# A two-pass channel-gating kernel: one load queue instead of two, and six rows kept in leftover SBUF

## The chip, the cores and the metric

The kernel runs on one core of a Trainium2 chip. The metric is the device time of one execution in microseconds (us), lower is better. A trace's span, from its first to its last instruction, is about 1.7 us shorter than the time of that execution. Executions fall into a fast and a slow state.

Names: PE is the matrix engine, DVE the vector engine, ACT the scalar engine, POOL and SP two more engines. SP and ACT issue the DMA transfers, each on a queue of its own. HBM is the memory outside the core; SBUF and PSUM are the memories on it. A queue's transfers are cut into packets, which the trace records one by one. "The trace's landing events" are the sixteen semaphore increments that end a transfer, one for each DMA engine; a transfer has landed with the last of them.

## The reference, cut to what matters

```python
def reference(x, w_down, w_up):          # x: (1, 256, 256, 384) bf16, 50.33 MB
    s = x.mean(axis=(1, 2))              # one mean per channel
    s = sigmoid(silu(s @ w_down) @ w_up) # w_down (384, 24), w_up (24, 384)
    return x * s[:, None, None, :]
```

No output element is known before all of x has been read, and x does not fit in SBUF. So some of x must be read twice.

## The kernel before

x is cut into 64 chunks of 1024 pixels: 128 partitions, 8 rows of 384 channels each, 0.786 MB. SBUF has room for 33 chunk buffers.

Pass 1 loads every chunk, and PE adds it to a running sum with eight matmuls against a matrix of ones. Even chunks are loaded by SP, odd ones by ACT. A buffer is loaded again when PE is done with it.

```python
# SP: even chunks (ACT has the same loop with range(1, NCH, 2))
for i in range(0, NCH, 2):
    b = bufof[i]                                  # i % 33
    if i >= nbuf:
        sp.wait_ge(sem_MM, i - nbuf + 1)          # PE has done with chunk i - 33
    sp.dma_start(bufs[b][:], x_rows(i, 0, K)).then_inc(sem_Lb[b], 16)
# ... ACT: the last chunk, 63, comes in two transfers, 6 rows and 2 rows (sem_LB)

# PE, strictly in the order of the chunks
pe.wait_ge(sem_G, 1); pe.wait_ge(sem_W, 32)       # weights; three small transposes
# ... three matmuls into ps_wT ...
for i in range(NCH):
    pe.wait_ge(sem_Lb[bufof[i]], 16 * load_cnt_at[i])
    for j in range(K):
        # ... at row 6 of the last chunk: pe.wait_ge(sem_LB, 16)
        mm = pe.matmul(ps_sum[:], ones_sb[:], bufs[b][:, j * C:(j + 1) * C], ...)
    mm.then_inc(sem_MM, 1)
```

Then six small steps on DVE, ACT and PE make the gate s. Pass 2 multiplies and stores: first the 33 chunks still in SBUF ("resident", 31 to 63), then chunks 0 to 30, each reread into a buffer whose store has landed. The first resident chunk goes out in quarters, so that the first store starts early.

```python
# SP: rereads
for j, i in enumerate(streamed2):                 # chunks 0..30
    sp.wait_ge(sem_STb[b], 16 * done_val[order2[j]])
    sp.dma_start(bufs[b][:], x_rows(i, 0, K)).then_inc(sem_Lb[b], 16)
# DVE: one multiply per unit; ACT: one store per unit
for (i, r0, r1) in units:
    # ... wait for the reread, if chunk i is one
    dve.tensor_tensor(buf3d(b, r0, r1), buf3d(b, r0, r1), s_bcast(r1 - r0), ALU.mult).then_inc(sem_MUL, 1)
```

Of the kernel before, what the change touches and what calls it, by code (L numbers as in the profile page):

```python
# [5 lines left out]

_MAX_BUFS = None
_K = 8


def bass_standalone__se_block__vision_kernel(
# [36 lines left out]
    with ExitStack() as ctx:  # L48
# [6 lines left out]
        def sem(name):  # L55
            return ctx.enter_context(nc.semaphore(name))
# [39 lines left out]
        def buf3d(n, r0=0, r1=K):  # L96
            return bufs[n][:].rearrange("p (k c) -> p k c", c=C)[:, r0:r1, :]

        def s_bcast(nrow):
            return s_sb[:].unsqueeze(1).to_broadcast([P, nrow, C])  # L100

        bufof = {i: i % nbuf for i in range(NCH)}
        resident = list(range(NCH - nbuf, NCH))
        streamed2 = list(range(0, NCH - nbuf))
        order2 = resident + streamed2
        buf2 = {}
        for i in resident:
            buf2[i] = bufof[i]
        for j, i in enumerate(streamed2):
            buf2[i] = buf2[order2[j]]  # L110

        last_split = K - 2 if NCH > 1 else K
        first2 = order2[0]
        p2_pieces = {i: [(0, K)] for i in order2}
        p2_pieces[first2] = [(r, r + K // 4) for r in range(0, K, K // 4)]

        lcnt = [0] * nbuf
        load_cnt_at = {}
# [9 lines left out]
            for (r0, r1) in p2_pieces[i]:  # L128
                units.append((i, r0, r1))
        scnt = [0] * nbuf  # L130
        store_cnt_after_unit = []
        for (i, r0, r1) in units:
            scnt[buf2[i]] += 1
            store_cnt_after_unit.append(scnt[buf2[i]])
        total_stores = list(scnt)
        done_val = {}
        n = 0
        for i in order2:
            n += len(p2_pieces[i])
            done_val[i] = store_cnt_after_unit[n - 1]  # L140

        last = NCH - 1

        with nc.Block() as block:

            @block.sync
            def _(sp):
                for i in range(0, NCH, 2):
                    b = bufof[i]
                    if i >= nbuf:  # L150
                        sp.wait_ge(sem_MM, i - nbuf + 1)
                    if i == last:
                        sp.dma_start(
                            buf3d(b, 0, last_split), x_rows(i, 0, last_split)
                        ).then_inc(sem_Lb[b], 16)
                        sp.dma_start(
                            buf3d(b, last_split, K), x_rows(i, last_split, K)
                        ).then_inc(sem_LB, 16)
                    else:
                        sp.dma_start(bufs[b][:], x_rows(i, 0, K)).then_inc(sem_Lb[b], 16)  # L160
                for j, i in enumerate(streamed2):
                    b = buf2[i]
                    sp.wait_ge(sem_STb[b], 16 * done_val[order2[j]])
                    sp.dma_start(bufs[b][:], x_rows(i, 0, K)).then_inc(sem_Lb[b], 16)

            @block.gpsimd
            def _(pool):
# [11 lines left out]
            @block.vector  # L179
            def _(dve):  # L180
                dve.memset(ones_sb[:], 1.0).then_inc(sem_C, 1)  # L181
                dve.memset(dummy_sb[:], 0.0).then_inc(sem_C, 1)  # L182

                dve.wait_ge(sem_MM, NCH)
                dve.wait_ge(sem_WT, 1)
                dve.tensor_tensor_reduce(  # L186
                    out=zscr_sb[:],
                    in0=wdnT_sb[:],
                    in1=ps_sum[0:R, :],
                    scale=inv_npix,  # L190
                    scalar=0.0,
                    op0=ALU.mult,
                    op1=ALU.add,
                    accum_out=z_sb[:],
                ).then_inc(sem_V2A, 1)
                dve.wait_ge(sem_A2V, 1)
                dve.tensor_scalar(  # L197
                    hb_sb[:], ones_sb[0:R, :], z_sb[:, 0:1], sig_sb[:, 0:1],
                    ALU.mult, ALU.mult,
                ).then_inc(sem_V2P, 1)  # L200

                dve.wait_ge(sem_A2V, 2)
                for (i, r0, r1) in units:
                    b = buf2[i]
                    if i in reread_cnt_at and r0 == 0:
                        dve.wait_ge(sem_Lb[b], 16 * reread_cnt_at[i])
                    dve.tensor_tensor(  # L207
                        buf3d(b, r0, r1), buf3d(b, r0, r1), s_bcast(r1 - r0), ALU.mult
                    ).then_inc(sem_MUL, 1)

            @block.tensor
            def _(pe):
                pe.wait_ge(sem_G, 1)
                pe.wait_ge(sem_W, 32)
                for c in range(CT):
                    mm = pe.matmul(  # L216
                        ps_wT[c][:], wdn_sb[:, c * R:(c + 1) * R], ident_sb[:],
                        start=True, stop=True,
                    )
                mm.then_inc(sem_T, 1)  # L220

                pe.wait_ge(sem_C, 2)
                for i in range(NCH):
                    b = bufof[i]
                    pe.wait_ge(sem_Lb[b], 16 * load_cnt_at[i])
                    nrow = last_split if i == last else K
                    for j in range(K):
                        if i == last and j == nrow:
                            pe.wait_ge(sem_LB, 16)
                        mm = pe.matmul(  # L230
                            ps_sum[:],
                            ones_sb[:],
                            bufs[b][:, j * C:(j + 1) * C],
                            start=(i == 0 and j == 0),
                            stop=(i == last and j == K - 1),
                        )
                    mm.then_inc(sem_MM, 1)

                pe.wait_ge(sem_V2P, 1)
                pe.matmul(  # L240
                    ps_u[:], hb_sb[:], wup_sb[:], start=True, stop=True
                ).then_inc(sem_P2A, 1)

            @block.scalar
            def _(act):
                act.dma_start(  # L246
                    wdn_sb[:].rearrange("p (k r) -> p k r", r=R),
                    w_down.rearrange("(k p) r -> p k r", p=P),
                ).then_inc(sem_W, 16)
                act.dma_start(wup_sb[:], w_up).then_inc(sem_W, 16)  # L250

                act.wait_ge(sem_C, 2)
                act.activation(dummy_sb[:, 1:2], dummy_sb[:, 0:1], ACT.Sigmoid)  # L253

                wdnT_done = [False]

                def emit_wdnT_copies():
                    act.wait_ge(sem_T, 1)
                    for c in range(CT):
                        ins = act.activation(  # L260
                            wdnT_sb[:, c * P:(c + 1) * P], ps_wT[c][:], ACT.Copy
                        )
                    ins.then_inc(sem_WT, 1)
                    wdnT_done[0] = True

                for i in range(1, NCH, 2):
                    b = bufof[i]
                    if i >= nbuf:
                        act.wait_ge(sem_MM, i - nbuf + 1)
                    if i == last:  # L270
                        act.dma_start(
                            buf3d(b, 0, last_split), x_rows(i, 0, last_split)
                        ).then_inc(sem_Lb[b], 16)
                        act.dma_start(
                            buf3d(b, last_split, K), x_rows(i, last_split, K)
                        ).then_inc(sem_LB, 16)
                    else:
                        act.dma_start(bufs[b][:], x_rows(i, 0, K)).then_inc(sem_Lb[b], 16)  # L278
                    if i == 7:
                        emit_wdnT_copies()  # L280
                if not wdnT_done[0]:
                    emit_wdnT_copies()

                act.wait_ge(sem_V2A, 1)
                act.activation(sig_sb[:], z_sb[:], ACT.Sigmoid).then_inc(sem_A2V, 1)  # L285

                act.wait_ge(sem_P2A, 1)
                act.activation(s_sb[:], ps_u[:], ACT.Sigmoid).then_inc(sem_A2V, 1)  # L288

                for n, (i, r0, r1) in enumerate(units):  # L290
                    b = buf2[i]
                    act.wait_ge(sem_MUL, n + 1)
                    act.dma_start(o_rows(i, r0, r1), buf3d(b, r0, r1)).then_inc(
                        sem_STb[b], 16
                    )
                for b in range(nbuf):
                    act.wait_ge(sem_STb[b], 16 * total_stores[b])

# [27 lines left out]
```

## Time and profile before

| | before |
|---|---|
| median time | 314.18 us (5 runs, 313.87 to 314.45) |
| span of the trace | 312.7 us |
| moved by DMA | 125.17 MB: 50.33 read, 24.4 read again, 50.33 written |
| end of the sum on PE | 128.4 us |
| first multiply of pass 2 | 130.5 us |

These lines are from the page of the kernel before: the busy tenths of the DMA engines and the rate in 40 equal slices of 7.8 us, then what was moved.

```profile
DMA  7999999999999998189999999999999999999997
GB/s 267 423 420 415 418 417 419 414 417 417 418 415 418 418 417 337 45 289 412 424 423 425 420 428 425 424 426 422 428 425 424 426 422 428 425 424 426 422 428 320
DMA packets 23914, 125.17 MB, mean 400 GB/s; under 512 B 3020, under 2 KB 3684, under 8 KB 23908
HBM read 74.75 MB, written 50.33 MB: 400 GB/s over the span
```

The DMA engines are full in both passes, at about 417 GB/s in pass 1 and 425 in pass 2, with a hole in slices 16 to 18. So time is bytes over rate, plus the hole. The hole is the only place where compute matters.

The chain of waits across the hole (start in us, length in us, what):

```profile
121.69 0.05 issue
121.73 6.69 PE ps_sum L230 x40
128.42 0.02 issue
128.44 0.54 DVE zscr_sb L186
...
129.99 0.50 ACT s_sb L288
130.49 0.02 issue
130.51 5.30 DVE xbuf L207 x6
```

The windows view of the kernel before: stretch in us, its length, busy time of PE, PE's weight load, DVE, ACT and POOL (with counts), granted PE clock, DMA share, GB/s.

```profile
120.00:125.00 5.00, 4.00 (x26) 2.19 (x25) 0.00 (x0) 0.00 (x0) 0.00 (x0) 1.00 0.75 297
125.00:128.50 3.50, 3.41 (x21) 1.85 (x19) 0.06 (x1) 0.00 (x0) 0.00 (x0) 1.00 0.01 5
128.50:131.00 2.50, 0.33 (x1) 0.09 (x1) 1.28 (x5) 0.69 (x2) 0.00 (x0) 1.00 0.00 0
134.50:138.00 3.50, 0.00 (x0) 0.00 (x0) 3.50 (x3) 0.00 (x0) 0.00 (x0) 0.50 0.86 248
```

DMA is all but done by 125 us, but PE works on, without a pause, to 128.4: forty matmuls in a row, five whole chunks, after the landing at 121.69. PE is not slow. Forty matmuls took 6.69 us; less the extra length of the last one (0.33 us from start to end, against a pitch of 0.163), that is 0.163 us each and 1.31 us to a chunk, while a chunk takes DMA 1.88 us. It is late because of what it had to wait for.

### The profile page before, as it was taken

How to read it: one execution, taken by the hardware profiler on the slowest of the kernel's cores; microseconds unless marked ns; L12 is line 12 of the kernel's file. 1: busy time of each engine (PE TensorE's matmuls, PEld its weight loads, DVE VectorE, ACT ScalarE, POOL GpSimd, SP SyncE). 2: the span in 40 equal slices, each digit the busy share in tenths (PEclk: the TensorE clock that was granted, in tenths of full speed). 3: DMA queues.
4: the chain of work that ended last, by engine and by line, in shares of the span. 5: the costliest groups of instructions: out<-in, count | busy, mean ns of one | idle time of the engine just before them, and what ended most of it. 6: DMA issues, size and time to landing. Idle time of an engine off the chain costs nothing.

```text
span 312.7 us, 1327 instructions
## 1 busy us (share of the span) xinstructions
PE 90.6 (29%) x516; PEld 48.2 (15%) x516; DVE 109.0 (35%) x72; ACT 2.8 (1%) x7; POOL 0.5 (0%) x5
## 2 busy tenths in 40 slices
PE   0777577777777777400000000000000000000000
PEld 0334333443443334200000000000000000000000
DVE  0000000000000000499999999999555540000000
ACT  1000000000000000000000000000000000000000
POOL 0000000000000000000000000000000000000000
PEclk9999999999999999955555555555555555555555
DMA  7999999999999998189999999999999999999997
GB/s 267 423 420 415 418 417 419 414 417 417 418 415 418 418 417 337 45 289 412 424 423 425 420 428 425 424 426 422 428 425 424 426 422 428 425 424 426 422 428 320
DMA packets 23914, 125.17 MB, mean 400 GB/s; under 512 B 3020, under 2 KB 3684, under 8 KB 23908
## 3 DMA queue, kind: packets, MB, share of 16 engines
q10 hardware_dynamic: 14836, 75.54, 58.7%
q1 hardware_dynamic: 9072, 49.55, 38.6%
q8 instruction: 4, 0.07, 0.1%
q14 instruction: 2, 0.02, 0.0%
HBM read 74.75 MB, written 50.33 MB: 400 GB/s over the span
## 4 chain that ended last, share of the span: by engine, by line
DMA 53%; DVE 26%; PE 2%; ACTq 1%; ACT 0%; issue 0%
DMA xbuf<-in_x_dram 39%; DVE xbuf L207 25%; DMA out_dram<-xbuf 12%; PE ps_sum L230 2%; DMA wup_sb<-in_w_up_dram 2%; ACTq L278 1%; DVE zscr_sb L186 0%; ACT wdnT_sb L260 0%; ACT s_sb L288 0%; PE ps_wT L216 0%; ACTq L246 0%; PE ps_u L240 0%; DVE hb_sb L197 0%; ACT sig_sb L285 0%; DVE z_sb L186 0%
## 5 line engine op out<-in xcount | busy, mean ns | idle before, releaser
L207 DVE TENSOR_TENSOR xbuf<-xbuf,s_sb 128x3072 bf16<-128x3072 bf16 (+1 forms) x67 | 108.0, 1679 | 20.4 <-DMA xbuf<-in_x_dram 19.4
L230 PE MATMUL ps_sum<-xbuf,ones 128*128 128x384 bf16 x512 | 89.9, 330 | 30.8 <-DMA xbuf<-in_x_dram 30.8
L230 PEld LDWEIGHTS ps_sum<-xbuf,ones 128*128 128x128 bf16 x512 | 47.9, 98 | 72.5 <-DMA xbuf<-in_x_dram 42.6
L186 DVE CUSTOM_DVE_ANT_0 zscr_sb<-wdnT_sb,ps_sum 24x384 f32<-24x384 bf16 x1 | 0.5, 542 | 127.4 <-PE ps_sum L230 127.4
L216 PE MATMUL ps_wT<-ident,wdn_sb 128*24 128x128 bf16 x3 | 0.5, 298 | 7.4 <-DMA wup_sb<-in_w_up_dram 7.4
L216 PEld LDWEIGHTS ps_wT<-ident,wdn_sb 128*24 128x24 bf16 x3 | 0.2, 112 | 7.4 <-issue 7.4
L253 ACT ACT_TABLE_LOAD x1 | 1.3, 1283 | 2.0 <-issue 2.0
L285 ACT ACTIVATE sig_sb<-z_sb 24x1 f32<-24x1 f32 x1 | 0.2, 202 | 120.5 <-DVE z_sb L186 120.5
L240 PE MATMUL ps_u<-wup_sb,hb_sb 24*128 24x384 bf16 x1 | 0.3, 332 | 1.2 <-DVE hb_sb L197 1.2
L260 ACT ACTIVATE wdnT_sb<-ps_wT 24x128 bf16<-24x128 f32 x3 | 0.6, 257 | 4.4 <-PE ps_wT L216 4.4
L288 ACT ACTIVATE s_sb<-ps_u 128x384 bf16<-128x384 f32 x1 | 0.5, 491 | 0.8 <-PE ps_u L240 0.8
L181 DVE MEMSET ones<- 128x128 bf16 x1 | 0.2, 165 | 0.9 <-PEq L311 0.9
L197 DVE TENSOR_SCALAR hb_sb<-ones,z_sb,sig_sb 24x128 bf16<-24x128 bf16 x1 | 0.3, 302 | 0.3 <-ACT sig_sb L285 0.3
L240 PEld LDWEIGHTS ps_u<-wup_sb,hb_sb 24*128 24x128 bf16 x1 | 0.1, 91 | 1.6 <-DVE hb_sb L197 1.6
L169 POOL TENSOR_SCALAR_AFFINE_SELECT ident<-ones 128x128 bf16<-128x128 bf16 x1 | 0.3, 294 | 0.6 <-DVE dummy_sb L182 0.6
L253 ACT ACTIVATE dummy_sb<-dummy_sb 128x1 f32<-128x1 f32 x1 | 0.2, 203 | 0.0
L311 POOL MEMSET const-bfloat16-1.0<- 128x1 bf16 x1 | 0.1, 102 | 0.0
L311 POOL MEMSET const-uint8-127<- 128x1 uint8 x1 | 0.1, 102 | 0.0
L311 POOL MEMSET const-float32-0.0<- 128x1 f32 x1 | 0.1, 99 | 0.3 <-issue 0.3
L311 POOL MEMSET const-float32-1.0<- 128x1 f32 x1 | 0.1, 99 | 0.0
L186 DVE DVE_READ_ACCUMULATOR2_ANT z_sb<- 24x1 f32 x1 | 0.1, 70 | 0.0
L182 DVE MEMSET dummy_sb<- 128x2 f32 x1 | 0.1, 60 | 0.0
## 6 DMA issues: line engine op xcount, KB each, us to landing
xbuf<-in_x_dram SPq DMA_DIRECT2D x63, 768.0 KB, 10.1
out_dram<-xbuf ACTq DMA_DIRECT2D x63, 768.0 KB, 23.0
xbuf<-in_x_dram ACTq DMA_DIRECT2D x31, 768.0 KB, 38.9
out_dram<-xbuf ACTq DMA_DIRECT2D x4, 192.0 KB, 2.0
xbuf<-in_x_dram ACTq DMA_DIRECT2D x1, 576.0 KB, 36.1
xbuf<-in_x_dram ACTq DMA_DIRECT2D x1, 192.0 KB, 33.2
wdn_sb<-in_w_down_dram ACTq DMA_DIRECT2D x1, 18.0 KB
wup_sb<-in_w_up_dram ACTq DMA_DIRECT2D x1, 18.0 KB
```

Of the source, the lines that this page charges most:

```text
L169: pool.affine_select(ident_sb[:], ones_sb[:], pattern=[[1, P]], compare_op=ALU.is_equal, fill=0.0, base=0, channel_multiplier=-1,).then_in ...
L186: dve.tensor_tensor_reduce(out=zscr_sb[:], in0=wdnT_sb[:], in1=ps_sum[0:R, :], scale=inv_npix, scalar=0.0, op0=ALU.mult, op1=ALU.add, accu ...
L197: dve.tensor_scalar(hb_sb[:], ones_sb[0:R, :], z_sb[:, 0:1], sig_sb[:, 0:1], ALU.mult, ALU.mult,).then_inc(sem_V2P, 1)
L207: dve.tensor_tensor(buf3d(b, r0, r1), buf3d(b, r0, r1), s_bcast(r1 - r0), ALU.mult).then_inc(sem_MUL, 1)
L216: mm = pe.matmul(ps_wT[c][:], wdn_sb[:, c * R:(c + 1) * R], ident_sb[:], start=True, stop=True,)
L230: mm = pe.matmul(ps_sum[:], ones_sb[:], bufs[b][:, j * C:(j + 1) * C], start=(i == 0 and j == 0), stop=(i == last and j == K - 1),)
L240: pe.matmul(ps_u[:], hb_sb[:], wup_sb[:], start=True, stop=True).then_inc(sem_P2A, 1)
L253: act.activation(dummy_sb[:, 1:2], dummy_sb[:, 0:1], ACT.Sigmoid)
L260: ins = act.activation(wdnT_sb[:, c * P:(c + 1) * P], ps_wT[c][:], ACT.Copy)
L278: act.dma_start(bufs[b][:], x_rows(i, 0, K)).then_inc(sem_Lb[b], 16)
L288: act.activation(s_sb[:], ps_u[:], ACT.Sigmoid).then_inc(sem_A2V, 1)
L311: nc = _bacc.Bacc("TRN2", target_bir_lowering=False, num_devices=1)
```

## The change

The change has three parts. All loads of pass 1 go through SP's queue, in order, meant to let chunks land in order. Leftover SBUF keeps six of the eight rows of chunk 30 through pass 1 (`xtra`), so that only two rows of it are reread. And the three transposes move behind chunk 8, so that PE starts when the first chunk is there. An option to leave buffers free for early rereads comes along, set to 0. Cut to its core:

```diff
+        XR = (nc.sbuf_bytes_remaining - 64) // (C * 2)      # 6 rows
+        XC = NCH - nbuf - 1                                 # chunk 30
+        xtra = sb("xtra", [P, XR * C], bf16)
...
+        p2_pieces[XC] = [(XR, K)]
+        units.insert(len(quarters), (-1, 0, XR))            # xtra goes out behind the four quarters
...
             def _(sp):
-                for i in range(0, NCH, 2):
+                for i in range(NCH):
...
+                    if i == XC:
+                        sp.dma_start(xtra3, x_rows(i, 0, XR)).then_inc(sem_XL, 16)
+                        sp.dma_start(buf3d(b, XR, K), x_rows(i, XR, K)).then_inc(sem_Lb[b], 16)
...
             def _(pe):
-                pe.wait_ge(sem_G, 1)
-                pe.wait_ge(sem_W, 32)
-                ... three transposes ...
                 for i in range(NCH):
...
+                    if i == tr_after:                       # chunk 8
+                        ... the three transposes ...
...
             def _(act):
-                for i in range(1, NCH, 2):
-                    ... odd chunks ...
```

More of the change, by code (lines that the diff above doesn't have):

```diff
@@ L8 @@
 _K = 8
+_FREE_BUFS = 0
 def bass_standalone__se_block__vision_kernel(
@@ L97, in buf3d @@
             return bufs[n][:].rearrange("p (k c) -> p k c", c=C)[:, r0:r1, :]
+        XR = (nc.sbuf_bytes_remaining - 64) // (C * 2)
+        XC = NCH - nbuf - 1
+        assert 0 < XR < K
+        xtra = sb("xtra", [P, XR * C], bf16)
+        xtra3 = xtra[:].rearrange("p (k c) -> p k c", c=C)
+        sem_XL = sem("sem_XL")
+        sem_XS = sem("sem_XS")
         def s_bcast(nrow):
@@ L102, in bass_standalone__se_block__vision_kernel @@
         bufof = {i: i % nbuf for i in range(NCH)}
-        resident = list(range(NCH - nbuf, NCH))
-        streamed2 = list(range(0, NCH - nbuf))
+        nfree = min(_FREE_BUFS, max(0, NCH - nbuf))
+        nres = nbuf - nfree if NCH > nbuf else nbuf
+        resident = list(range(NCH - nres, NCH))
+        streamed2 = list(range(0, NCH - nres))
+        free_bufs = {}
+        for i in range(NCH - nres):
+            free_bufs[bufof[i]] = i
+        for i in resident:
+            free_bufs.pop(bufof[i], None)
         order2 = resident + streamed2
-        buf2 = {}
-        for i in resident:
-            buf2[i] = bufof[i]
+        buf2 = {i: bufof[i] for i in resident}
+        free_list = sorted(free_bufs.items())
+        reread_src = {}
         for j, i in enumerate(streamed2):
-            buf2[i] = buf2[order2[j]]
+            if j < len(free_list):
+                b, lastch = free_list[j]
+                buf2[i] = b
+                reread_src[i] = ("mm", lastch + 1)
+            else:
+                prev = order2[j - len(free_list)]
+                buf2[i] = buf2[prev]
+                reread_src[i] = ("store", prev)
+        last = NCH - 1
         last_split = K - 2 if NCH > 1 else K
-        first2 = order2[0]
         p2_pieces = {i: [(0, K)] for i in order2}
-        p2_pieces[first2] = [(r, r + K // 4) for r in range(0, K, K // 4)]
+        quarters = [(r, r + K // 4) for r in range(0, K, K // 4)]
+        p2_pieces[order2[0]] = quarters
+        assert XC == streamed2[-1]
+        p2_pieces[XC] = [(XR, K)]
         lcnt = [0] * nbuf
@@ L130, in bass_standalone__se_block__vision_kernel @@
         scnt = [0] * nbuf
-        store_cnt_after_unit = []
+        done_val = {}
         for (i, r0, r1) in units:
             scnt[buf2[i]] += 1
-            store_cnt_after_unit.append(scnt[buf2[i]])
+            done_val[i] = scnt[buf2[i]]
         total_stores = list(scnt)
-        done_val = {}
-        n = 0
-        for i in order2:
-            n += len(p2_pieces[i])
-            done_val[i] = store_cnt_after_unit[n - 1]
-        last = NCH - 1
+        units.insert(len(quarters), (-1, 0, XR))
         with nc.Block() as block:
@@ L151, in _ @@
                         sp.wait_ge(sem_MM, i - nbuf + 1)
-                    if i == last:
+                    if i == XC:
+                        sp.dma_start(xtra3, x_rows(i, 0, XR)).then_inc(sem_XL, 16)
+                        sp.dma_start(
+                            buf3d(b, XR, K), x_rows(i, XR, K)
+                        ).then_inc(sem_Lb[b], 16)
+                    elif i == last and last_split < K:
                         sp.dma_start(
@@ L160, in _ @@
                         sp.dma_start(bufs[b][:], x_rows(i, 0, K)).then_inc(sem_Lb[b], 16)
-                for j, i in enumerate(streamed2):
+                for i in streamed2:
                     b = buf2[i]
-                    sp.wait_ge(sem_STb[b], 16 * done_val[order2[j]])
-                    sp.dma_start(bufs[b][:], x_rows(i, 0, K)).then_inc(sem_Lb[b], 16)
+                    kind, v = reread_src[i]
+                    if kind == "mm":
+                        sp.wait_ge(sem_MM, v)
+                    else:
+                        sp.wait_ge(sem_STb[b], 16 * done_val[v])
+                    if i == XC:
+                        sp.dma_start(
+                            buf3d(b, XR, K), x_rows(i, XR, K)
+                        ).then_inc(sem_Lb[b], 16)
+                    else:
+                        sp.dma_start(bufs[b][:], x_rows(i, 0, K)).then_inc(sem_Lb[b], 16)
             @block.gpsimd
@@ L203, in _ @@
                 for (i, r0, r1) in units:
+                    if i < 0:
+                        dve.tensor_tensor(
+                            xtra3, xtra3, s_bcast(XR), ALU.mult
+                        ).then_inc(sem_MUL, 1)
+                        continue
                     b = buf2[i]
-                    if i in reread_cnt_at and r0 == 0:
+                    if i in reread_cnt_at and (r0, r1) == p2_pieces[i][0]:
                         dve.wait_ge(sem_Lb[b], 16 * reread_cnt_at[i])
@@ L212, in _ @@
             def _(pe):
-                pe.wait_ge(sem_G, 1)
-                pe.wait_ge(sem_W, 32)
-                for c in range(CT):
-                    mm = pe.matmul(
-                        ps_wT[c][:], wdn_sb[:, c * R:(c + 1) * R], ident_sb[:],
-                        start=True, stop=True,
-                    )
-                mm.then_inc(sem_T, 1)
-                pe.wait_ge(sem_C, 2)
+                pe.wait_ge(sem_C, 1)
+                tr_after = min(8, last)
                 for i in range(NCH):
@@ L225, in _ @@
                     pe.wait_ge(sem_Lb[b], 16 * load_cnt_at[i])
-                    nrow = last_split if i == last else K
+                    if i == XC:
+                        pe.wait_ge(sem_XL, 16)
                     for j in range(K):
-                        if i == last and j == nrow:
+                        if i == last and j == last_split:
                             pe.wait_ge(sem_LB, 16)
@@ L232, in _ @@
                             ones_sb[:],
-                            bufs[b][:, j * C:(j + 1) * C],
+                            (xtra if i == XC and j < XR else bufs[b])[
+                                :, j * C:(j + 1) * C
+                            ],
                             start=(i == 0 and j == 0),
@@ L237, in _ @@
                     mm.then_inc(sem_MM, 1)
+                    if i == tr_after:
+                        pe.wait_ge(sem_G, 1)
+                        pe.wait_ge(sem_W, 32)
+                        for c in range(CT):
+                            mm = pe.matmul(
+                                ps_wT[c][:], wdn_sb[:, c * R:(c + 1) * R],
+                                ident_sb[:], start=True, stop=True,
+                            )
+                        mm.then_inc(sem_T, 1)
                 pe.wait_ge(sem_V2P, 1)
@@ L253, in _ @@
                 act.activation(dummy_sb[:, 1:2], dummy_sb[:, 0:1], ACT.Sigmoid)
-                wdnT_done = [False]
-                def emit_wdnT_copies():
-                    act.wait_ge(sem_T, 1)
-                    for c in range(CT):
-                        ins = act.activation(
-                            wdnT_sb[:, c * P:(c + 1) * P], ps_wT[c][:], ACT.Copy
-                        )
-                    ins.then_inc(sem_WT, 1)
-                    wdnT_done[0] = True
-                for i in range(1, NCH, 2):
-                    b = bufof[i]
-                    if i >= nbuf:
-                        act.wait_ge(sem_MM, i - nbuf + 1)
-                    if i == last:
-                        act.dma_start(
-                            buf3d(b, 0, last_split), x_rows(i, 0, last_split)
-                        ).then_inc(sem_Lb[b], 16)
-                        act.dma_start(
-                            buf3d(b, last_split, K), x_rows(i, last_split, K)
-                        ).then_inc(sem_LB, 16)
-                    else:
-                        act.dma_start(bufs[b][:], x_rows(i, 0, K)).then_inc(sem_Lb[b], 16)
-                    if i == 7:
-                        emit_wdnT_copies()
-                if not wdnT_done[0]:
-                    emit_wdnT_copies()
+                act.wait_ge(sem_T, 1)
+                for c in range(CT):
+                    ins = act.activation(
+                        wdnT_sb[:, c * P:(c + 1) * P], ps_wT[c][:], ACT.Copy
+                    )
+                ins.then_inc(sem_WT, 1)
                 act.wait_ge(sem_V2A, 1)
@@ L290, in _ @@
                 for n, (i, r0, r1) in enumerate(units):
+                    act.wait_ge(sem_MUL, n + 1)
+                    if i < 0:
+                        act.dma_start(o_rows(XC, 0, XR), xtra3).then_inc(sem_XS, 16)
+                        continue
                     b = buf2[i]
-                    act.wait_ge(sem_MUL, n + 1)
                     act.dma_start(o_rows(i, r0, r1), buf3d(b, r0, r1)).then_inc(
@@ L295, in _ @@
                     )
+                act.wait_ge(sem_XS, 16)
                 for b in range(nbuf):
```

## The prediction

> **What bounds the kernel now.** The DMA engines, in two passes with a hole between. The page's slices show them full from 3 to 123 us at about 417 GB/s (pass 1, load and sum) and from 140 to 310 us at about 425 GB/s (pass 2, multiply and store, with 31 of 64 chunks read a second time); 125.17 MB move in all. No compute engine is near its limit. In the chain of waits, 40 matmuls (6.69 us) run from 121.73 to 128.42 us; then 2.1 us of small steps make s, and the first multiply starts at 130.51. The windows view shows DMA falling from 393 GB/s at 122 us to 52 at 124.5-125 and nothing between 126 and 131.5.
>
> **Why PE ends so late.** A chunk is 8 matmuls at 163 ns (16 take 2.77 us with the last one's tail), about 1.31 us, against 1.88 us per chunk of DMA. PE is faster than the loads and should end just behind them. The landing events of the trace show why it does not: odd chunks (ACT queue) land later than the even ones (SP queue). Chunk 59 lands at 121.69, after chunk 60 (119.67); 61 at 124.13, after 62 (123.43); 63's two parts at 125.58 and 126.02. PE works in order, so five chunks are left at 121.7 and it ends 2.4 us after the last landing.
>
> **What the change does.**
> 1. All loads of pass 1 go through SP in order. Chunks then land in order, and PE should end about 0.4 us after the last landing (two rows, about 0.5 us of matmul) instead of 2.4. That saves 2.0 us if the last landing stays at 126.0. The 16 engines finish raggedly now (rate falls from 123.0, last byte 125.7); if one queue also evens that, up to 4.2. I take 2.7. I expect no loss of rate: the Trainium skill, "DMA: Bandwidth & Descriptors", section "Issuing engines are not separate DMA queues", says that several issuers save only issue time. The trace agrees as far as it goes: SP alone read at 395 to 418 GB/s between 2.5 and 4 us, and ACT alone stores at 425 GB/s from 257 to 305 us. An SP issue takes about 0.33 us unblocked, so one issuer keeps up with 1.88 us per chunk.
> 2. Leftover SBUF holds 6 of 8 rows of chunk 30, so 0.59 MB is not read again: 0.59 MB / 425 GB/s = 1.39 us, all on the critical path since pass 2 is bound by bytes from end to end.
> 3. The extra multiply (6 rows, about 1.32 us) goes before the first full chunk, so its store starts 0.4 us sooner, in the idle 134.5-135.0; but the next store then waits for DVE. Worth about 0.1 us.
> 4. Transposes move behind chunk 8; PE starts at about 5 instead of 7.8 us. Worth nothing: PE waits for loads anyway. The zero-valued free-buffer option changes nothing.
>
> Sum: 2.7 + 1.4 + 0.1 = 4.2 us. Predicted 309.9 us, range 307.9 to 311.7. Chances: faster by over 2% 0.11, within 2% 0.88, slower 0.01.
>
> **What would show it.** HBM read falls by 0.59 MB to 74.16 MB. The chain's last PE piece has at most two chunks and ends at 124.5 to 126.5 us. Slices of pass 1 stay at 415-420 GB/s. First multiply at 126.5 to 128.7. Pass 2, from first multiply to the end, takes 180.7 us instead of 182.2.
>
> **What would make it wrong.** One queue reading at another rate than two: 1% is 1.2 us. The engines' raggedness growing or going. The slow stretch when loads join the stores (135-330 GB/s at 136.5-139.5) changing length, since the second reread now waits for a store queued later.

## The result, and the profile after

The median fell from 314.14 us (13 runs) to 311.10 us (7 runs, 311.02 to 311.30), by 3.0 us. The ratio is 0.9906, with a 95% interval from 0.9896 to 0.9916. Here and below a ratio is the mean time of one kernel's fast runs over that of the kernel before's fast runs of the same rounds, so it is not quite the ratio of the medians quoted.

The same views of the changed kernel. First its page:

```profile
DMA  7999999999999999199999999999999999999997
GB/s 282 420 419 415 418 418 417 412 415 418 419 416 418 419 418 380 58 303 426 424 426 423 424 423 426 424 426 424 426 424 426 425 422 426 424 425 425 426 424 314
HBM read 74.16 MB, written 50.33 MB: 402 GB/s over the span
```

The rates are as before, from one queue alone in pass 1 as from two. HBM read fell by 0.59 MB, as predicted.

The chain of waits across the hole:

```profile
123.82 0.05 issue
123.86 3.16 PE ps_sum L263 x16
127.03 0.02 issue
127.05 0.54 DVE zscr_sb L221
...
128.60 0.50 ACT s_sb L310
129.10 0.02 issue
129.12 1.96 DVE xbuf L247 x4
131.08 1.27 DVE xtra L240
```

Two chunks of matmuls instead of five stand at the end. But PE ends at 127.03, not between 124.5 and 126.5 as predicted, and the first multiply starts at 129.12, not by 128.7.

The windows:

```profile
120.00:125.00 5.00, 4.44 (x23) 2.10 (x24) 0.00 (x0) 0.00 (x0) 0.00 (x0) 0.85 0.71 284
125.00:128.50 3.50, 2.28 (x12) 0.99 (x10) 0.85 (x3) 0.20 (x1) 0.00 (x0) 0.85 0.00 2
128.50:131.00 2.50, 0.06 (x1) 0.00 (x0) 1.88 (x4) 0.49 (x1) 0.00 (x0) 0.65 0.16 58
134.50:138.00 3.50, 0.00 (x0) 0.00 (x0) 3.50 (x3) 0.00 (x0) 0.00 (x0) 0.50 0.96 241
```

This profiled execution was granted a PE clock of 0.85 in pass 1 where the kernel before had 1.00. Its mean clock is 0.652; the seven other executions have 0.708 to 0.713, like the kernel before (0.713). Its 16 last matmuls took 3.16 us here; at full clock the experiments below show 2.85 to 2.90. So this profile overstates PE's end by about 0.3 us, and its time, 311.30, is the longest of the seven counted. Of the difference, 1.4 us (128.42 to 127.03) lie in pass 1 by this profile, and 1.7 us in pass 2, from the first multiply to the end of the span (182.2 us before, 180.5 after, with spans of 312.7 and 309.6).

### The profile page after: what moved, and what is told of

The parts are those of the page before. It is cut to its first block, busy times and chain, and to the rows that moved or that the text cites. A ratio compares the mean times of both kernels' runs of the same rounds, so it can differ in the third digit from the quotient of the medians.

```text
span 309.6 us, 1332 instructions
## 1 busy us (share of the span) xinstructions
PE 107.5 (35%) x516; PEld 48.1 (16%) x516; DVE 109.2 (35%) x73; ACT 2.8 (1%) x7; POOL 0.5 (0%) x5
## 4 chain that ended last, share of the span: by engine, by line
DMA 43%; DVE 25%; SPq 11%; PE 2%; issue 1%; ACT 0%
DMA xbuf<-in_x_dram 31%; DVE xbuf L247 25%; DMA out_dram<-xbuf 12%; SPq L186 11%; PE ps_sum L263 2%; DVE xtra L240 0%; DVE zscr_sb L221 0%; ACT s_sb L310 0%; PE ps_u L284 0%; DVE hb_sb L232 0%; ACT sig_sb L307 0%; DVE z_sb L221 0%
## 5 line engine op out<-in xcount | busy, mean ns | idle before, releaser
L263 PE MATMUL ps_sum<-xbuf,ones 128*128 128x384 bf16 x506 | 105.8, 360 | 19.6 <-DMA xbuf<-in_x_dram 19.6
L221 DVE CUSTOM_DVE_ANT_0 zscr_sb<-wdnT_sb,ps_sum 24x384 f32<-24x384 bf16 x1 | 0.5, 542 | 126.0 <-PE ps_sum L263 126.0
L263 PE MATMUL ps_sum<-xtra,ones 128*128 128x384 bf16 x6 | 1.3, 352 | 0.3 <-DMA xbuf<-in_x_dram 0.3
L240 DVE TENSOR_TENSOR xtra<-xtra,s_sb 128x2304 bf16<-128x2304 bf16 x1 | 1.3, 1349 | 0.0
```

The lines of the kernel that those rows point to most:

```text
L221: dve.tensor_tensor_reduce(out=zscr_sb[:], in0=wdnT_sb[:], in1=ps_sum[0:R, :], scale=inv_npix, scalar=0.0, op0=ALU.mult, op1=ALU.add, accu ...
L240: dve.tensor_tensor(xtra3, xtra3, s_bcast(XR), ALU.mult).then_inc(sem_MUL, 1)
L263: mm = pe.matmul(ps_sum[:], ones_sb[:], (xtra if i == XC and j < XR else bufs[b])[:, j * C:(j + 1) * C], start=(i == 0 and j == 0), stop=( ...
```

## The experiments

All experiments passed the check of the result, even e6, which leaves rows out of the sum. Line numbers L... differ from kernel to kernel.

### The parts alone: one queue (e1), kept rows (e2), transposes undone (e5)

e1 is the kernel before with only this edit; the transposes stay first.

```diff
-                for i in range(0, NCH, 2):      # SP
+                for i in range(NCH):
...
-                for i in range(1, NCH, 2):      # ACT: its loop of loads goes
```

> The kernel before with one part of the change alone: all loads of pass 1 on the SP queue, in order; transposes still first, no rows kept. Theory (the two parts simply add): PE ends about 1.4 us earlier than before (127.0 instead of 128.4 us), pass 2 keeps its 182.2 us, total about 312.7 us. Rival (the whole 3.0 us comes from the bytes and what they shift in pass 2, and PE ends early only because it starts early): no change, 314.1 us.

Measured: 312.84 us against 313.94 of the kernel before, ratio 0.996 (0.9947 to 0.9972). PE's last stretch, from the timeline of PE:

```profile
122.11 1.48 PE L230 MATMUL ps_sum<-xbuf,ones 128*128 128x384 bf16 x8 [0.41 <-DMA xbuf<-in_x_dram]
124.00 2.90 PE L230 MATMUL ps_sum<-xbuf,ones 128*128 128x384 bf16 x16 [0.41 <-DMA xbuf<-in_x_dram]
```

PE ended at 126.90, 1.5 us earlier than before, and pass 2 took 182.1 us, as before. The expectation held, and the rival fell.

e2 is the kernel before with the kept rows alone (the `xtra` lines of the diff above), on two queues.

> The kernel before with the other part alone: six rows of chunk 30 kept in leftover SBUF, loads still on two queues, transposes still first. Theory: 0.59 MB less at 425 GB/s is 1.4 us, plus up to 0.3 us at the start of pass 2; PE still ends near 128.4; total about 312.5 us. Rival (pass 2 is not bound by bytes to its end): under 0.7 us, so above 313.4 us.

Measured: 312.00 against 313.94, ratio 0.9933 (0.9919 to 0.9947). Pass 2 took 180.5 us, 1.7 less than before, as expected. PE also ended at 127.65 instead of 128.41, which was not expected. Chunk 30 now comes in two transfers on SP's queue, 256 smaller packets instead of 128. Up to chunk 27 each odd chunk landed about 5.5 us after the even chunk before it; at chunk 29 it was 4.5 us, and from chunk 31 on 1.5 us, so that by the end of the pass the chunks of the two queues land in order (table below; why smaller packets do this is seen under e8). So e2 has part of the gain of pass 1 as well, and the two parts alone do not divide the gain cleanly. Their drops in the medians, 1.10 and 1.94 us, happen to come to that of the whole change; by the ratios they are 1.26 and 2.10, together 3.4 against 2.95 us.

e5 is the changed kernel with the transposes first again.

> The changed kernel with its third part undone: the three transposes stand first on PE again, so PE starts at about 7.5 instead of 5.5 us. Theory (PE catches up long before the end of pass 1): no change against the changed kernel, 311.1 us. Rival (the early start of PE is part of the gain): up to 2 us more, 312 to 313 us.

Measured: 310.98 us (ratio 0.9892, 0.9879 to 0.9906), against 0.9906 of the changed kernel. PE started at 7.61 instead of 5.47 us and ended no later (126.59). The third part is worth nothing, as predicted.

### Is it the order? PE in the order of landing (e3)

```diff
-                for i in range(NCH):
+                pe_order = list(range(NCH - 5)) + [last - 3, last - 4, last - 1, last - 2, last]
+                for i in pe_order:
```

> The kernel before, two queues, only that PE takes the last five chunks in the order in which they land (60, 59, 62, 61, 63). Theory (PE's lag is its order against the landing order): five chunks no longer wait for chunk 59; PE has about 1.3 us of work behind the last landing minus what two rows cost, and ends at about 127.4 to 127.6 us instead of 128.4; total about 313.2 us. Rival (one queue helps because the DMA moves data better): no change, 314.1 us.

Measured: 313.34 us, ratio 0.9976 (0.9963 to 0.9988). The timeline of PE:

```profile
117.47 5.37 PE L231 MATMUL ps_sum<-xbuf,ones 128*128 128x384 bf16 x32 [1.00 <-DMA xbuf<-in_x_dram]
123.35 4.08 PE L231 MATMUL ps_sum<-xbuf,ones 128*128 128x384 bf16 x24 [0.51 <-DMA xbuf<-in_x_dram]
```

Three chunks are left instead of five, and PE ends at 127.43 as expected. No transfer was touched. So PE's end moves by 1.0 us, of the 1.5 that one queue gained, without any better use of the DMA engines: what counts is how much of PE's work is still undone at the last landing.

### Two queues made level (e4, e8, e10)

If only the lag of the odd chunks was at fault, two level queues should do as well as one.

e4 issues ACT's first two chunks ahead of the weights:

```diff
+                for i in (1, 3):
+                    act.dma_start(bufs[i][:], x_rows(i, 0, K)).then_inc(sem_Lb[i], 16)
                 act.dma_start(wdn_sb ...)
                 act.dma_start(wup_sb ...)
```

> The kernel before, two queues, only that ACT issues its first two chunk loads ahead of the two small weight loads. Theory (the ACT queue is behind only because its first chunk waits for the weights; the two queues then share evenly for the rest of the pass): odd chunks land about one chunk time earlier relative to the even ones, in order, and PE ends about 1 us earlier; total about 313.1 us. Rival (the ACT queue is served less): the odd chunks lag as before, 314.1 us.

Measured: 315.29 us, ratio 1.0042 (1.0029 to 1.0054): slower. The weights landed only at 17.3 us, where they had landed at 7.25, and the wait for them held up PE's start (17.8 us) and ACT's later loads. By the end odd chunks lagged further than before. I took ACT's wait for the cause, and its queue to have run dry; e8 shows that neither was so.

e8 also puts the transposes behind chunk 8 and the copies that depend on them behind all of ACT's loads.

> The kernel before with two queues made level: ACT issues its first two chunks ahead of the weights, and the transposes stand behind chunk 8 with their copies behind all of ACT's loads, so that neither PE nor ACT waits for the weights early on. Theory (a lag of the ACT queue, not two queues as such, made PE late; the earlier attempt moved the weights behind the chunks but left ACT waiting for them[...]): chunks land in order, PE ends at about 127.0, total as with one queue, 312.8 us. Rival (two queues always lag): 313.5 us or more.

Measured: 315.57 us, ratio 1.0037 (1.0024 to 1.0051). The timeline of PE:

```profile
120.07 9.28 PE L221 MATMUL ps_sum<-xbuf,ones 128*128 128x384 bf16 x56 [0.76 <-DMA xbuf<-in_x_dram]
```

Seven chunks were left at 120.07. The packets of the trace, by queue, show why. ACT had issued the weights at 1.7 and 2.2 us, behind two chunks, and three further chunk loads by 4.7 us. Its queue moved the two chunks until 10.4 us and then w_down, which is 384 packets of 48 bytes. These went one for one with SP's packets of 6,144 bytes: from 10.5 to 15.5 us ACT's queue moved 352 packets of 48 bytes, SP's queue 323 of 6,144 bytes and 32 of 4 bytes, at 400 GB/s. The last small packets went at 16.2 us; the chunks behind them began at 16.0. Chunks 1 and 3 had landed 0.4 and 0.5 us after chunks 0 and 2; chunk 5 landed 8.0 us after chunk 4, and the later odd chunks lagged by 10 to 12 us for most of the pass.

So the two queues take turns by the packet, whatever its size. ACT's queue was never empty; it spent its turns on 18 KB. The packets of e4 show the same, with the same 352 and 323 between 10.5 and 15.5 us. PE's wait and ACT's wait for the weights, which I had blamed after e4, are gone in e8 and were not the cause of the lag. In the kernel before the weights stand first: SP's queue moves its first chunk packet at 1.8 us, ACT's at 6.0 us, and its chunks land about 6 us after SP's from the start. Turns by the packet also explain e2: chunk 30, in twice as many packets, cost SP's queue twice the turns, and ACT's queue gained about one chunk on it (between 60 and 61 us SP's queue moved 53 packets, 50 of them of 1,536 bytes, and ACT's 49 of 6,144).

e10 lets POOL issue the two weight loads, so that ACT's queue has chunks alone; all else is as in e8.

```diff
             def _(pool):
+                pool.dma_start(wdn_sb ..., w_down ...).then_inc(sem_W, 16)
+                pool.dma_start(wup_sb[:], w_up).then_inc(sem_W, 16)
```

> The kernel before with two queues and the small weight loads taken off the ACT queue altogether (POOL issues them); transposes behind chunk 8, copies behind all of ACT's loads. [...] Theory (the lag of odd chunks comes from the weight loads standing in that queue, and PE's late end from the lag): the queues stay level, PE ends at about 127.0, total about 312.8 us. Rival (the ACT queue falls behind without them too): odd chunks lag, 313.9 us or more.

Measured: 313.73 against 314.02, ratio 0.9989 (0.9975 to 1.0003): no gain clear of noise. Now the queues are level: w_down went as 16 packets of 1,152 bytes on a queue of POOL's, and each odd chunk landed 0.2 to 0.5 us after the even one before it. Still PE ends at 128.11, not at 127.0. The timeline of PE:

```profile
122.03 2.77 PE L226 MATMUL ps_sum<-xbuf,ones 128*128 128x384 bf16 x16 [0.98 <-DMA xbuf<-in_x_dram]
125.34 2.77 PE L226 MATMUL ps_sum<-xbuf,ones 128*128 128x384 bf16 x16 [0.53 <-DMA xbuf<-in_x_dram]
```

So both sides of this dispute fell. The odd chunks' lag did come from the weights in their queue (rival wrong), but level queues are not as good as one (theory wrong). Two level queues land their chunks in pairs: 60 and 61 at 121.99 and 122.46, 62 and the six rows of 63 at 125.29 and 125.46. The Trainium skill, "DMA: Bandwidth & Descriptors", section "Queues, rings and completion order", says that each DMA engine serves its queues in turn, packet by packet; the pairs agree with that, 0.2 to 0.5 us apart where one queue lands chunks 1.9 us apart. Two transfers that share the engines both finish at the end of their common time, and PE gets its last two chunks at once.

### The end of pass 1 as a sum

This suggests a rule without any word on queues. PE takes chunks in its order; each starts 0.04 us after its landing or when PE is free, and costs 0.163 us a row; the last row's end comes 0.16 us later. The three constants are read from the kernel before (121.69 to 121.73; 6.69 us for 40; 0.33 less 0.163). With each trace's landing events, the rule gives PE's end:

| run | chunk 59 | 60 | 61 | 62 | 63, 6 rows | 63, 2 rows | PE end by the rule | measured |
|---|---|---|---|---|---|---|---|---|
| before | 121.69 | 119.67 | 124.13 | 123.43 | 125.58 | 126.02 | 128.41 | 128.41 |
| after (clock 0.85) | 118.20 | 120.08 | 121.95 | 123.82 | 125.22 | 125.70 | 126.72 | 127.01 |
| one queue (e1) | 118.29 | 120.17 | 122.06 | 123.95 | 125.38 | 125.82 | 126.88 | 126.90 |
| kept rows, two queues (e2) | 119.16 | 121.39 | 122.91 | 124.83 | 125.36 | 125.84 | 127.64 | 127.65 |
| PE order (e3) | 121.21 | 119.52 | 124.03 | 123.31 | 125.47 | 125.90 | 127.42 | 127.43 |
| weights behind (e4) | 121.92 | 116.43 | 123.82 | 120.20 | 125.25 | 125.69 | 129.36 | 129.35 |
| e8 | 121.91 | 116.43 | 123.83 | 120.20 | 125.24 | 125.69 | 129.35 | 129.34 |
| level queues (e10) | 118.69 | 121.99 | 122.46 | 125.29 | 125.46 | 125.95 | 128.10 | 128.11 |

(In e4 and e8 PE's last stretch begins earlier, with chunk 57, which landed at 120.03 and 120.02.) The kernel before gave the constants, so it is no test; the others agree within 0.02 us wherever the granted clock was full at the end of pass 1, and so do the five runs that are not in the table and sum every row (e5, e7, e9, e11, e12). The profile of the changed kernel misses by 0.29 us, and it is the one at a clock of 0.85. The last landing itself hardly moves: it lies between 125.7 and 126.0 in all eight kernels. So what one queue buys is mainly that the landings are spread evenly, not that they end sooner (0.2 us of 1.5 in e1).

### What is still left at the end of PE (e6)

Wrong result: PE sums one row of chunk 62 and three rows of chunk 63 only, each after its landing.

```diff
-                    for j in range(K):
+                    rows = range(K)
+                    if i == last - 1:
+                        rows = [0]
+                    if i == last:
+                        rows = [0, last_split, K - 1]
+                    for j in rows:
```

> Wrong result on purpose: the changed kernel, but PE sums only one row of chunk 62 and three rows of chunk 63 (after each part's landing), so that almost no PE work is left behind the last loads. Theory (the last two chunks land only 1.9 us apart in all and hold 2.6 us of matmuls, so PE still ends about 1.1 us after the last landing, not 0.4): the lag becomes about 0.4 us, the time falls by 0.6 to 0.8 us, to about 310.4 us. Rival (the lag is the time from a landing to the first matmul that uses it): no change, 311.1 us.

Measured: 310.74 us, ratio 0.9883 (0.9868 to 0.9898); e5 of the same rounds, with all matmuls, had 310.98. The timeline of PE:

```profile
123.88 0.34 PE L268 MATMUL ps_sum<-xbuf,ones 128*128 128x384 bf16 x1 [0.40 <-DMA xbuf<-in_x_dram]
125.28 0.98 PE L268 MATMUL ps_sum<-xbuf,ones 128*128 128x384 bf16 x3 [1.06 <-DMA xbuf<-in_x_dram]
```

PE ended at 126.26, 0.55 us behind the last landing (125.71). With all matmuls it is 1.08 us behind (e1), so the work in the tail is worth about 0.5 us in the traces. In the times only 0.24 us show against e5, in whose profile the last landing came 0.16 us earlier (why is not known); the intervals overlap, so the size in the times is not settled. The direction agrees with the theory; the expected 0.6 to 0.8 us was too much.

### The hole and the bytes (e7)

```diff
-_FREE_BUFS = 0
+_FREE_BUFS = 2
...
-        XC = NCH - nbuf - 1
+        XC = NCH - nbuf - 1 + _FREE_BUFS
```

> The changed kernel with two buffers set free (the option that the change brings and leaves at 0): two rereads stand in the queue right behind pass 1 and run in the idle stretch between the passes, but two chunks fewer stay resident, so 1.57 MB more is read, 3.7 us at 425 GB/s. Theory A (bytes are bytes): the hole takes the two extra chunks and the sum is zero, 311.1 us. Theory B (the slow stretch where rereads join the stores, which costs about 1.6 us, comes from loads starting beside stores): it also goes, 309.6 us. Rival C (the hole cannot be used): 314.8 us.

Measured: 310.89 us, ratio 0.9892 (0.9879 to 0.9906). HBM read rose to 75.73 MB, by 1.57 MB. The windows view:

```profile
125.00:128.50 3.50, 2.29 (x13) 0.98 (x11) 0.85 (x3) 0.20 (x1) 0.00 (x0) 1.00 0.70 285
128.50:131.00 2.50, 0.13 (x1) 0.00 (x0) 1.81 (x4) 0.49 (x1) 0.00 (x0) 1.00 0.16 60
134.50:138.00 3.50, 0.00 (x0) 0.00 (x0) 3.50 (x3) 0.00 (x0) 0.00 (x0) 0.50 0.93 230
```

The hole now carries 285 GB/s where it carried 2, and the time is the same: theory A. Here the hole between the passes can be filled only with bytes that a resident chunk would have saved. The slow stretch from 134.5 to 138 is still there (230 GB/s, before 248, after 241), so theory B falls. What makes this stretch slow, when rereads first join the stores, stays open. It costs about 1.5 us (an estimate: 3.5 us at 230 to 248 GB/s instead of 425).

### Trying to go further (e11, e9, e12)

e11 loads w_down with 144 contiguous bytes to a partition instead of three times 48:

```diff
-                    w_down.rearrange("(k p) r -> p k r", p=P),
+                    w_down.rearrange("(p k) r -> p k r", p=P),
...
-                        wdnT_sb[:, c * P:(c + 1) * P], ps_wT[c][:], ACT.Copy
+                        wdnT_sb[:].rearrange("r (p k) -> r k p", k=CT)[:, c, :],
+                        ps_wT[c][:], ACT.Copy,
```

> The changed kernel, only that w_down is loaded with 144 contiguous bytes to a partition instead of three pieces of 48 (row 3p+k instead of 128k+p, undone by the copies' write pattern). Theory: 256 of 384 small packets of about 36 ns go, 16 to an engine, 0.58 us of each engine early in pass 1, so that pass 1 ends 0.4 to 0.6 us earlier: 310.6 us. Rival (these packets hide in the slow start of pass 1, where the engines are not full): no change, 311.1 us.

Measured: 311.14 us, ratio 0.9904 (0.989 to 0.9917). No change: the last landing stayed at 125.76. The rival was right in the number, but not in its reason: between 3 and 6 us DMA did move more (409 GB/s against 360), and had moved less before 3 us (76 against 113); the second cancels the first but for 0.1 us. Why it moved less is not known.

e9 adds to that 34 whole buffers and one extra row, by laying `wdnT_sb` over rows of `s_sb` and sending the unused product of the reduction to PSUM:

```diff
-        wdnT_sb = sb("wdnT_sb", [R, C], bf16)
-        zscr_sb = sb("zscr_sb", [R, C], fp32)
         s_sb = sb("s_sb", [P, C], bf16)
+        wdnT_sb = s_sb[0:R, :]
...
-                    out=zscr_sb[:],
+                    out=ps_u[0:R, :],
```

> A version meant to beat both: the changed kernel with the plain weight load, and with two small tiles laid over others that are free at that time, which makes room for 34 whole buffers and one row instead of 33 and six rows. Reread bytes fall by another 0.375 chunk, 0.29 MB, 0.69 us at 425 GB/s. With the plain weights' 0 to 0.6 us: 309.9 to 310.4 us. Rival (the smaller extra piece opens a gap among the first stores): 0.3 us worse than that.

Measured: 311.11 us (310.48 to 311.46), ratio 0.9901 (0.9886 to 0.9916), inconclusive. It read 0.30 MB less (73.86 MB), but pass 2 took 180.2 us, 0.3 less than e11's 180.5 where 0.7 were expected. By 20 us after the first multiply it had moved 6.72 MB, e11 6.84 MB; at 425 GB/s that is 0.3 us, about what the rival said of the smaller extra piece.

e12 keeps another 1.5 chunks in PSUM, in six tiles beside two for the sum and the small products. The Trainium skill, "PSUM — Partial Sum Buffer", section "Specifications (TRN2)", says that VectorE reads PSUM in any data type but writes it rightly in 4-byte types, so the bf16 rows are copied as 32-bit words with a bitwise OR of the word with itself, and read as bf16. The result was correct, which agrees; a bf16 write was not tried.

```diff
+        ps_keep = [ps(f"ps_keep{n}", [P, 512]) for n in range(6)]
+        KEEP = {10: (0, 8), 11: (8, 4)}            # chunk: (first row of ps_keep, rows)
...                                                # DVE, in pass 1, two rows at a time:
+                        src = bufs[b][:, r * C:(r + 2) * C].bitcast(u32)
+                        ins = dve.tensor_tensor(ps_keep[...][:, 0:C].bitcast(u32), src, src, ALU.bitwise_or)
...                                                # SP waits for the copy before it reloads those buffers,
...                                                # and skips the rereads; DVE, in pass 2:
+                            kept = ps_keep[...][:, 0:C].bitcast(bf16)
+                            ins = dve.tensor_tensor(buf3d(b, r, r + 2), kept.rearrange("p (k c) -> p k c", c=C), s_bcast(2), ALU.mult)
```

> A version meant to beat both: the changed kernel with another 1.5 chunks kept on the chip. DVE, idle in pass 1, copies chunk 10 and four rows of chunk 11 into six PSUM banks (as 32-bit words, so that no value changes), and in pass 2 multiplies them from there into the buffers that their rereads would have filled. 1.18 MB less is read again. Theory (pass 2 is bound by bytes, 425 GB/s): 2.8 us less than the changed kernel, 308.3 us, pass 2 at about 177.7 us. Rival (the missing rereads or slower multiplies from PSUM leave the DMA short of work for a while): 309.5 to 311 us.

Measured: 308.28 us (308.16 to 308.34), ratio 0.9818 (0.9805 to 0.9831) against the kernel before: 5.7 us less than before, and 2.8 less than the changed kernel. From its page and from the view of the tile `ps_keep` (operation and count: shortest, median and longest in ns, first and last start in us, shapes):

```profile
HBM read 72.98 MB, written 50.33 MB: 402 GB/s over the span
```

```profile
L240 DVE TENSOR_TENSOR ps_keep<-xbuf x6: 559/560/567, 24.6 to 26.9; 128x384 uint32<-128x384 uint32 x6
L280 DVE TENSOR_TENSOR xbuf<-ps_keep,s_sb x6: 550/550/553, 202.1 to 204.4; 128x768 bf16<-128x768 bf16 x6
```

Six copies of 0.56 us in a pass in which DVE is idle, and six multiplies as fast as those from SBUF (0.554 us for the same shape), remove 1.18 MB. At 425 GB/s that is 2.8 us, and 2.8 were measured. This version beats both.

## Why the prediction was right or wrong

The range, 307.9 to 311.7, held the result, 311.1, and "within 2%" was right. The middle, 309.9, was 1.2 us too low: pass 1 gained 1.2 to 1.3 us less than counted and pass 2 about 0.2 more, so that the range held also because it was 3.8 us wide. Point by point:

- **The bound** was right. e7 and e12 confirm it from two sides: in pass 2 time follows the bytes at 425 GB/s.
- **Item 1, landings in order**: the mechanism was right (e3 shows it without touching a transfer), its size was not. The prediction took 2.7 us; the profiles show 1.4 us, and 1.5 at full clock (e1). The step that failed is "PE should end about 0.4 us after the last landing (two rows, about 0.5 us of matmul)". Even in order, chunk 62 lands only 1.88 us before the last landing, and the first six rows of chunk 63 only 0.44 to 0.48 us before it. From the landing of chunk 62 on, PE has 16 matmuls to do, 2.6 us. The lag was 1.08 us in e1 and 1.31 in the profile at the lower clock. The prediction had checked that PE is faster than DMA over a chunk, and then treated PE as having no backlog at all at the end.
- The same item counted on part of the raggedness of the DMA engines to go ("up to 4.2. I take 2.7"). It did not: the last landing moved from 126.02 to 125.70, and the fall of the rate at the end of pass 1 stayed.
- **No loss of rate on one queue** was right: 412 to 420 GB/s in the full slices of pass 1, before 414 to 423. The skill's statement that several issuers only save issue time held for the rate. It does not cover when each transfer ends, and that is where this change earned its share of pass 1 (e10).
- **Item 2, kept rows, 1.39 us**: right in kind, a little low. HBM read fell by exactly 0.59 MB; pass 2 fell by 1.7 us (1.4 by bytes). The surplus lies in the first 20 us of pass 2, where the changed kernel had moved 6.86 MB and the kernel before 6.66, though it rereads less; 0.2 MB are 0.5 us at 425 GB/s. **Item 3** had put 0.1 us there. e1 also gained part of this (6.82 MB by then) without kept rows, so its cause is not settled.
- **Item 4** was right: e5 shows no loss with the transposes first.
- What the prediction gave as signs: HBM read, the last PE piece of two chunks, the slices (to 3 GB/s) and pass 2 (180.5 against 180.7) came true; the end of PE (127.03 against at most 126.5) and the first multiply (129.12 against at most 128.7) did not, and they point at the term that was too large.

## What to carry to other kernels

When a barrier waits for a consumer of streamed loads, the time that counts is the consumer's work still undone at the last landing. Compute it from the landing times of the last few transfers: that the consumer is faster on average says little. Two queues that share the DMA engines moved no more bytes here than one, but made their transfers land in pairs and late; a single queue spaced the landings evenly, so issue in the order of use. The two queues took turns by the packet, so 18 KB in small packets set one of them back by more than a chunk: keep such loads off a queue of large ones. Where a pass is bound by bytes, a byte kept on chip is worth about its transfer time (e12; e9 got less than half of it), and idle PSUM filled by an idle engine is room for it.

## What the Trainium skill lacked or had wrong

- "DMA: Bandwidth & Descriptors", section "Issuing engines are not separate DMA queues", says that issuing from several engines saves only issue time. It lacks that two queues change when transfers land: with two level queues the last whole chunk landed at 125.29 us and PE ended at 128.11, with one at 123.95 and 126.90, at the same rate.
- The same page, section "Bandwidth", gives 425 GB/s for a 16 MB load (issued from GpSimd). Here loads alone ran at about 417 GB/s over 100 us, from one queue as from two, and stores alone at 425.
- No page works out what small packets cost a queue that shares the engines with another: issued by ACT, w_down's 384 packets of 48 bytes went one for one with SP's packets of 6,144 bytes and took from 10.4 to 16.2 us (e8); issued by POOL, it went as 16 packets of 1,152 bytes between 6.1 and 7.1 us (e10).
- No page has the slow stretch when loads join running stores: 230 to 248 GB/s over 3.5 us, in the kernel before, in the changed one and with two rereads taken out of it (e7).
- "PSUM — Partial Sum Buffer" does not mention PSUM as a place to keep input data. Here 128x768 bf16 were copied there in 0.56 us and multiplied from there in 0.55 us, as fast as from SBUF.
